# Reordering the start-up of a fused attention and gated-unit kernel: two load queues, evacuations between normalisations, casts behind masks

## The chip, the cores and the metric

One core of a Trainium2 chip runs the whole kernel. The metric is the time of one execution in microseconds (us), as the device reports it; a profiled execution gives the span, some 1.8 us shorter. The kernel before took 198.24 us (median of 3 runs, 197.85 to 199.29). Single runs of one kernel differ by about 1% here, and some fall in a slower state; ratios use fast runs alone.

## The reference, cut to what matters

```python
# q, k, v: (8 batches, 8 heads, 576, 64) float32
scores = scale * np.matmul(q, k.transpose(0, 1, 3, 2))
scores = np.where(pos[:, None] // 64 >= pos[None, :] // 64, scores, -1e9)   # block-causal
attn   = softmax(scores)                        # over the last axis
x      = (attn @ v), heads side by side         # (8, 576, 512)
gate   = sigmoid(causal convolution of x with 5 taps per channel)
out    = (gate * (x @ w_val)) @ w_out           # w_val, w_out: (512, 512)
```

## The kernel before

The program is software-pipelined by hand: nothing is reordered by a scheduler, each engine runs its instructions in the order in which the source emits them, and a tile layer adds the semaphores. A step `p` is one pair of heads (32 steps, 4 per batch). It computes the scores of pair `p`, the value products of pair `p - 1`, the transposes of pair `p + 1`, and from step 5 on parts of the gated unit of an earlier batch (convolution, `val`, and output tiles).

576 positions are 4 blocks of 128 and a *tail* of 64. The tails of all 8 heads of a batch are loaded together, cast to fp16 by GpSimd (`cast_tails`), transposed by TensorE (`trans_tails`) and evacuated by VectorE, once in 4 steps. The other pieces are the mask and the order of emission:

```python
def mask(p):                       # zeroes the forbidden corners of exp(scores)
    pt = pts[p % NPT]              # written by ScalarE's exponential (line 188)
    nc.gpsimd.memset(pt[64:128, ...], 0.0)
    nc.gpsimd.memset(pt[64:128, 0:2, 896:960], 0.0)

def casts(p):                      # all on GpSimd, ahead of mask(p)
    for i in (p + 1, p + 2):
        if i < NP and i not in qkT and i not in qk16 and (p >= 5 or i == p + 1):
            cast_qk(i)
    cast_v(p)
    if p % 4 == 0:
        cast_vtail(p // 4)
    if p == 3 or (p > 0 and p % 4 == 0 and p + 4 < NP):
        cast_tails((p + 4) // 4, nc.gpsimd)
    if p in (6, 7):
        cast_w_out(p - 6)

for p in range(NP):
    # ... (cv: a step with a convolution) ...
    loads(p)
    casts(p)
    s_tile(p, 0)                   # scores: matmuls, then one exponential each
    s_tile(p, 1)
    # ... p == 0 cut ...
    av(p - 1, ...)                 # value products and normalisation, both heads
    trans(p + 1, 2)                # 8 transposes (TensorE), evacuation (VectorE)
    # ... out(3) from step 11; permutations of w_out ...
    s_tile(p, 2)
    mask(p)
    # ... s_last, conv ...
    xtrans(p - 1, ...)
    # ... scale_w_val in steps 5 and 6, val twice ...
    if p == 3 or (p > 0 and p % 4 == 0 and p + 4 < NP):
        trans_tails((p + 4) // 4, 1)     # last thing of TensorE's step
```

The softmax here doesn't subtract the row's maximum and nothing guards it: scores larger than these inputs give would overflow.

## Time and profile before

| stretch | TensorE busy | step length | what it does |
|---|---|---|---|
| 0 to 8 us | partly, with fillers | | first loads, casts, transposes |
| 8 to 31 us, steps 0 to 4 | 8.1 of 10 us from 20 to 30 us | 3.7 to 4.3 us from step 1 | attention alone |
| 31 to 67 us, steps 5 to 11 | 8.4 to 9.2 of 10 us | 4.4 to 6.5 us | attention and gated unit, no output until step 11 |
| 67 to 166 us, steps 12 to 31 | all of it | 4.7 to 5.7 us | all stages |
| 166 to 197 us | nearly all of it | | remaining gates and outputs |

A step's length is taken here from the start of its first exponential on ScalarE to the start of the next step's, read off the timeline. From the page of the kernel before, the 40-slice rows (each digit is a busy share in tenths; PEclk is the granted TensorE clock) and the chain that ended last:

```profile
PE   2999878779899999999999999999999999999992
...
PEclk9999999999999999999999999999999999999998
DMA  5999999999899568876887687977775111124445
...
PE 80%; DVE 10%; POOL 3%; ACT 2%; DMA 2%; issue 1%; POOLq 0%; SPq 0%; DVEq 0%; ACTq 0%
```

TensorE is full from about a third of the way, and the chain is 80% TensorE. In the first third it is not, and DMA is at 9 tenths there.

### The profile page before, as it was taken

Reading aid. Unit: us, or ns where it says so; the run is one execution under the profiler, and the core shown is the slowest. Engines: PE = TensorE matmul, PEld = TensorE weight load, DVE = VectorE, ACT = ScalarE, POOL = GpSimd, SP = SyncE. Lnnn points to the kernel's source line nnn. Section 1 sums busy time; section 2 is a strip of 40 time slices with the busy share of each in tenths; the row PEclk is TensorE's granted clock in tenths of the full one; section 3 lists DMA queues with packets and bytes.
Section 4 is the critical chain, followed back from the end, with each engine's and each line's share of the span. In section 5 each row is a group of like instructions: output and inputs, shape, how many; then the busy total and the mean of one; then the engine's idle time right before and its main releaser. Section 6 shows DMA issues by size and latency. Waiting matters only on the chain.

```text
span 196.6 us, 8730 instructions
## 1 busy us (share of the span) xinstructions
PE 183.3 (93%) x3714; PEld 124.4 (63%) x3714; DVE 130.8 (67%) x286; ACT 138.6 (71%) x192; POOL 83.5 (42%) x168
## 2 busy tenths in 40 slices
PE   2999878779899999999999999999999999999992
PEld 1456656557577676667766677677767676755550
DVE  4346785897678686777686877768676868642451
ACT  4438778758699778877888878887988787635321
POOL 7363664596444554345434644464445422100000
PEclk9999999999999999999999999999999999999998
DMA  5999999999899568876887687977775111124445
GB/s 155 256 286 265 250 274 323 312 215 278 242 224 253 171 174 217 255 228 186 236 232 234 189 240 212 276 216 207 220 213 146 57 56 58 58 107 165 163 160 213
DMA packets 70337, 40.43 MB, mean 206 GB/s; under 512 B 48149, under 2 KB 64789, under 8 KB 70298
## 3 DMA queue, kind: packets, MB, share of 16 engines
q1 hardware_dynamic: 69872, 39.46, 73.8%
q8 instruction: 29, 0.48, 1.0%
q10 hardware_dynamic: 426, 0.40, 0.6%
q14 instruction: 10, 0.08, 0.2%
HBM read 30.42 MB, written 9.44 MB: 203 GB/s over the span
## 4 chain that ended last, share of the span: by engine, by line
PE 80%; DVE 10%; POOL 3%; ACT 2%; DMA 2%; issue 1%; POOLq 0%; SPq 0%; DVEq 0%; ACTq 0%
PE G L33 51%; PE S L33 18%; PE G L154 6%; PE G L244 5%; DVE qkT L165 3%; DVE x L235 3%; DMA vs<-in_v_dram 2%; POOL qk L129 1%; ACT pt L188 1%; PE G L141 1%; DVE w_val L379 1%; DVE rc L234 1%; DVE gv L282 1%; POOL v L134 1%; POOL pt L204 1%
## 5 line engine op out<-in xcount | busy, mean ns | idle before, releaser
L188 ACT ACTIVATE pt<-S 128x1024 f16<-128x1024 f32 x96 | 95.0, 1024 | 21.4 <-PE S L33 19.1
L204 POOL MEMSET pt<- 64x384 f16 x32 | 13.5, 423 | 74.0 <-ACT pt L188 73.9
L33 PE MATMUL G<-xt,w_val 128*128 128x288 f16 x256 | 37.9, 286 | 0.3 <-DVE qkT L165 0.2
L165 DVE COPY qkT<-G 128x1024 f16<-128x1024 f16 x31 | 37.7, 1215 | 0.2 <-PE G L154 0.2
L129 POOL CAST qk<-qks 128x1024 f16<-128x1024 f32 x31 | 32.9, 1061 | 10.9 <-DMA qks<-in_k_dram 7.7
L33 PEld LDWEIGHTS <-pt 128*128 128x128 f16 x960 | 31.2, 97 | 8.6 <-issue 4.0
L33 PE MATMUL G<-w_out,gv 128*128 128x512 f16 x144 | 36.5, 379 | 0.0
L33 PE MATMUL G<-v,pt 128*128 128x65 f16 x896 | 34.1, 194 | 1.7 <-DVE gv L282 1.3
L282 DVE SCALAR_TENSOR_TENSOR gv<-th,G 128x288 f16<-128x288 f32 x64 | 28.2, 453 | 10.7 <-PE G L33 9.0
L304 ACT COPY osb<-G 128x512 f32<-128x512 f32 x31 | 18.2, 586 | 23.8 <-PE G L33 22.0
L235 DVE TENSOR_TENSOR x<-G,rc 128x320 f16<-128x320 f32 x64 | 31.5, 492 | 2.2
L33 PEld LDWEIGHTS <-qkT 64*128 64x128 f16 x496 | 16.0, 94 | 22.9 <-issue 16.8
L33 PE MATMUL S<-qkT 64*128 64x512 f16 (+1 forms) x248 | 28.5, 301 | 2.1 <-DVE qkT L165 1.1
L33 PEld LDWEIGHTS <-w_val 128*128 128x128 f16 x256 | 24.2, 98 | 8.5 <-issue 0.9
L234 DVE RECIPROCAL rc<-G 128x5 f32<-128x5 f32 x64 | 12.2, 190 | 22.6 <-PE G L33 22.5
L246 DVE COPY xt<-G 128x576 f16<-128x576 f16 x32 | 14.6, 455 | 13.5 <-PE G L244 13.2
L154 PE MATMUL G<-ident,qk 128*128 128x128 f16 x256 | 20.1, 222 | 0.2 <-POOL qk L129 0.2
L134 POOL CAST v<-vs 128x512 f16<-128x512 f32 x32 | 19.9, 621 | 0.5 <-DMA vs<-in_v_dram 0.3
L33 PEld LDWEIGHTS <-gv 128*128 128x128 f16 x144 | 12.9, 98 | 9.9
L33 PE MATMUL G<-xt,DG 32*32 32x288 f16 x640 | 17.2, 288 | 0.0
L33 PE MATMUL S<-xt,DG 32*32 32x288 f16 x640 | 17.1, 287 | 0.0
L154 PEld LDWEIGHTS <-qk 128*128 128x128 f16 x256 | 15.4, 100 | 1.3 <-POOL qk L129 0.4
(58 smaller groups left out, 151.8 us busy)
## 6 DMA issues: line engine op xcount, KB each, us to landing
out_dram<-osb SPq DMA_DIRECT2D x35, 256.0 KB, 2.1
qks<-in_q_dram SPq DMA_DIRECT2D x32, 256.0 KB, 4.2
vs<-in_v_dram SPq DMA_DIRECT2D x64, 128.0 KB, 4.4
qks<-in_k_dram SPq DMA_DIRECT2D x31, 256.0 KB, 4.3
tlst<-in_q_dram SPq DMA_DIRECT2D x8, 128.0 KB, 4.8
tlst<-in_k_dram SPq DMA_DIRECT2D x8, 128.0 KB, 4.6
vtst<-in_v_dram SPq DMA_DIRECT2D x8, 128.0 KB, 4.8
w_st<-in_moe_w_val_dram SPq DMA_DIRECT2D x2, 512.0 KB, 6.3
```

The costliest lines, as they stand in the source:

```text
L33: nc.tensor.matmul(out=out, lhsT=lhsT, rhs=rhs, start=start, stop=stop, skip_group_check=True)
L129: nc.gpsimd.tensor_copy(out=o, in_=s)
L134: nc.gpsimd.tensor_copy(out=v16s[p % NV][0:128, 0:4, 0:2, 0:64], in_=s)
L154: nc.tensor.transpose(out=r[:, o:o + 128], in_=t[0:128, c, 2 * i:2 * i + 2, 0:64], identity=ident16[0:128, 0:128])
L165: nc.vector.tensor_copy(out=o[0:128].rearrange("p i (s n) -> p i s n", n=4), in_=src)
L188: nc.scalar.activation(out=pts[p % NPT][0:128, 0:2, 512 * t:512 * t + 512], in_=s[0:128, 0:2, 0:512], func=AF.Exp, bias=0.0, scale=0.125)
L204: nc.gpsimd.memset(pt[64:128, 0:2, 0:1536].rearrange("p h (t s) -> p h t s", t=3)[:, :, :, 0:64], 0.0)
L234: nc.vector.reciprocal(out=rc[0:128], in_=O[:, :, 64:65])
L235: nc.vector.tensor_tensor(out=x[0:128, 0:5, h, 0:64], in0=O[:, :, 0:64], in1=rc[0:128].to_broadcast([128, 5, 64]), op=ALU.mult)
L246: nc.vector.tensor_copy(out=xts[b % NX][0:128, g, 4:4 + SEQ], in_=r[:, 0:SEQ])
L282: nc.vector.scalar_tensor_tensor(out=gv[u][0:128, x, bi, hf, 0:288], in0=t[0:128, x, 0:288], scalar=1.0, in1=r[0:128, 0:288], op0=ALU.add, ...
L304: nc.scalar.copy(out=o[0:128], in_=r[0:128, 0:512])
```

## The change

Intent: begin earlier and keep VectorE and GpSimd from holding TensorE in the first third. The parts are: first loads on two queues and the first transposes in two PSUM banks; in steps 1 to 4 the evacuation of the transposes between the two normalisations; query/key casts only one tile ahead until step 9; tail and weight casts behind the mask; tail loads later; gate matmuls spread over the step, output tiles from step 12 instead of 11.

```diff
+    load_tails(0)                       # k half now on ScalarE's queue
+    nc.scalar.dma_start(out=conv_nat[0:5, 0:512], in_=moe_conv_w[:, :])
+    load_v1(0, nc.scalar)
     tiny = const([128, 1], fp32, "tiny")
... cut: casts of tile 0 both on VectorE, transposes of tile 0 in banks 2 and 0,
... av() split into av() and norm(), conv() with the score bank's tanh first
     def loads(p):
-        if b + 2 < B and m == 2:
+        if b + 2 < B and m == 3 and b > 0:
             load_tails(b + 2)
...
+    def tails(p):
+        if p in (3, 7):
+            return p // 3
+        return p // 4 + 1 if p > 4 and p % 4 == 0 and p + 4 < NP else None
+
     def casts(p):
...
-            if ... (p >= 5 or i == p + 1):
+            if ... (p >= 9 or i == p + 1):
...
-        if p == 3 or (p > 0 and p % 4 == 0 and p + 4 < NP):
-            cast_tails((p + 4) // 4, nc.gpsimd)
-        if p in (6, 7):
-            cast_w_out(p - 6)
+
+    def mask_and_tails(p):
+        mask(p)
+        if tails(p):
+            cast_tails(tails(p), nc.gpsimd)
+        if p in (7, 8):
+            cast_w_out(p - 7)
...
+    for p in range(LAG):                # steps 0 to 4
...
+        if p > 1:
+            xtrans(p - 2, 3)
+        av(p - 1, 0, 0)
+        norm(p - 1, 0, 0)
+        av(p - 1, 1, 1)
+        trans(p + 1, 2)
+        norm(p - 1, 1, 1)
+        s_tile(p, 2)
+        mask_and_tails(p)
...
+        if tails(p):
+            trans_tails(tails(p), 0)    # still at the end of the same step
... cut: steps 5 to 31 likewise; scale_w_val 0 to 3 all in step 6; fillers 26 -> 13
```

More of the change, by code (lines that the diff above doesn't have):

```diff
@@ L94, in load_tails @@
         for o, src in ((0, q), (64, k)):
-            nc.sync.dma_start(out=t[o:o + 64, 0:8, 0:64],
+            (nc.scalar if b == 0 and o else nc.sync).dma_start(
+                              out=t[o:o + 64, 0:8, 0:64],
                               in_=src[b, 0:8, 512:576, 0:64].rearrange("h s d -> s h d"))
@@ L100, in load_vtail, with load_v1 @@
                           in_=v[b, 0:8, 512:576, 0:64].rearrange("h s d -> s h d"))
-    def load_v1(p):
+    def load_v1(p, eng=None):
         b, g = divmod(p, 4)
@@ L105, in load_v1 @@
         for h in range(2):
-            nc.sync.dma_start(
+            (eng or nc.sync).dma_start(
                 out=t[0:128, 0:4, h, 0:64],
@@ L125, in cast_qk @@
         if first:
-            nc.scalar.copy(out=o[:, 0:2], in_=s[:, 0:2])
+            nc.vector.tensor_copy(out=o[:, 0:2], in_=s[:, 0:2])
             nc.vector.tensor_copy(out=o[:, 2:4], in_=s[:, 2:4])
@@ L148, in trans @@
     def trans(p, bank=None):
-        r = gbank(bank)[0:128].bitcast(fp16)
         t = qk16.pop(p)
+        banks = (2, 0) if p == 0 else (bank, bank)
+        rr = [GT[i][0:128].bitcast(fp16) for i in banks]
         for i in range(2):
@@ L153, in trans @@
                 o = 512 * i + 128 * c
-                nc.tensor.transpose(out=r[:, o:o + 128], in_=t[0:128, c, 2 * i:2 * i + 2, 0:64],
+                nc.tensor.transpose(out=rr[i][:, o:o + 128], in_=t[0:128, c, 2 * i:2 * i + 2, 0:64],
                                     identity=ident16[0:128, 0:128])
-        src = r.rearrange("p (i n s) -> p i s n", i=2, n=4)
+        src = [r.rearrange("p (i n s) -> p i s n", i=2, n=4) for r in rr]
         if p == 0:
             o = [const([128, 512], fp16, f"qk0_{i}")[0:128] for i in range(2)]
-            nc.scalar.copy(out=o[0].rearrange("p (s n) -> p s n", n=4), in_=src[:, 0])
-            nc.vector.tensor_copy(out=o[1].rearrange("p (s n) -> p s n", n=4), in_=src[:, 1])
+            nc.scalar.copy(out=o[0].rearrange("p (s n) -> p s n", n=4), in_=src[0][:, 0])
+            nc.vector.tensor_copy(out=o[1].rearrange("p (s n) -> p s n", n=4), in_=src[1][:, 1])
             qkT[p] = o
@@ L164, in trans @@
             qkT[p] = [o[0:128, i] for i in range(2)]
-            nc.vector.tensor_copy(out=o[0:128].rearrange("p i (s n) -> p i s n", n=4), in_=src)
+            nc.vector.tensor_copy(out=o[0:128].rearrange("p i (s n) -> p i s n", n=4), in_=src[0])
     def s_tile(p, t):
@@ L211, with av @@
     x16 = {}
-    def av(p, banks):
+    def av(p, h, bank):
         b, g = divmod(p, 4)
@@ L216, in av, with norm, avs @@
         vv = v16s[p % NV]
-        x = p2.tile([128, 5, 2, 64], fp16, tag="x16", name="x16")
-        x16[p] = x
-        for h in range(2):
-            r = gbank(banks[h])
-            for i in range(5):
-                for j in range(i + 1):
-                    if j == 4:
-                        o = 64 * (4 * h + g)
-                        l = pt4[b % 2][0:128].rearrange("p a s -> p (a s)")[:, o:o + 128]
-                        w = v16t[b % 2][0:128, 2 * g + h, 0:65]
-                    else:
-                        o = 1280 + 64 * j if i == 4 else off[j] + 128 * i
-                        l = pt[0:128, h, o:o + 128]
-                        w = vv[0:128, j, h, 0:65]
-                    mm(r[0:128, 65 * i:65 * i + 65], l, w, start=(j == 0), stop=(j == i))
-            O = r[0:128, 0:325].rearrange("p (i d) -> p i d", d=65)
-            rc = p2.tile([128, 5, 1], fp32, tag="rc", name="rc")
-            nc.vector.reciprocal(out=rc[0:128], in_=O[:, :, 64:65])
-            nc.vector.tensor_tensor(
-                out=x[0:128, 0:5, h, 0:64], in0=O[:, :, 0:64],
-                in1=rc[0:128].to_broadcast([128, 5, 64]), op=ALU.mult)
+        r = gbank(bank)
+        for i in range(5):
+            for j in range(i + 1):
+                if j == 4:
+                    o = 64 * (4 * h + g)
+                    l = pt4[b % 2][0:128].rearrange("p a s -> p (a s)")[:, o:o + 128]
+                    w = v16t[b % 2][0:128, 2 * g + h, 0:65]
+                else:
+                    o = 1280 + 64 * j if i == 4 else off[j] + 128 * i
+                    l = pt[0:128, h, o:o + 128]
+                    w = vv[0:128, j, h, 0:65]
+                mm(r[0:128, 65 * i:65 * i + 65], l, w, start=(j == 0), stop=(j == i))
+    def norm(p, h, bank):
+        if h == 0:
+            x16[p] = p3.tile([128, 5, 2, 64], fp16, tag="x16", name="x16")
+        O = GT[bank][0:128, 0:325].rearrange("p (i d) -> p i d", d=65)
+        rc = p2.tile([128, 5, 1], fp32, tag="rc", name="rc")
+        nc.vector.reciprocal(out=rc[0:128], in_=O[:, :, 64:65])
+        nc.vector.tensor_tensor(
+            out=x16[p][0:128, 0:5, h, 0:64], in0=O[:, :, 0:64],
+            in1=rc[0:128].to_broadcast([128, 5, 64]), op=ALU.mult)
+    def avs(p, banks):
+        for h in range(2):
+            av(p, h, banks[h])
+            norm(p, h, banks[h])
     def xtrans(p, bank=None):
@@ L249, with conv @@
     th = {}
-    def conv(n, banks=(None, None)):
+    def conv(n, banks=(None, None), score_first=False):
         b, hf = divmod(n, 2)
@@ L264, in conv @@
                        start=(kk == 0), stop=(kk == 4))
-        for row in (2, 3):
-            nc.scalar.activation(out=t[0:128, row, 0:288], in_=rr[row][:, 0:288],
-                                 func=AF.Tanh, bias=0.0, scale=0.5)
-        nc.scalar.activation(out=t[0:128, 0:2, 0:288], in_=s[0:128, 0:2, 0:288],
-                             func=AF.Tanh, bias=0.0, scale=0.5)
+        for part in ((0, 2, 3) if score_first else (2, 3, 0)):
+            if part == 0:
+                nc.scalar.activation(out=t[0:128, 0:2, 0:288], in_=s[0:128, 0:2, 0:288],
+                                     func=AF.Tanh, bias=0.0, scale=0.5)
+            else:
+                nc.scalar.activation(out=t[0:128, part, 0:288], in_=rr[part][:, 0:288],
+                                     func=AF.Tanh, bias=0.0, scale=0.5)
     def val(n, x, bank=None):
@@ L311 @@
     nc.scalar.activation(out=tiny[0:128], in_=tiny[0:128], func=AF.Exp, bias=0.0, scale=1.0)
-    nc.scalar.dma_start(out=conv_nat[0:5, 0:512], in_=moe_conv_w[:, :])
-    load_tails(0)
     make_identity(nc, ident)
+    wz = const([128, 512], fp16, "wz")
+    nc.vector.memset(wz[0:128], 0.0)
     nc.vector.tensor_copy(out=ident16[0:128], in_=ident[0:128])
@@ L321 @@
     load_qk1(1)
-    load_v1(0)
     load_vtail(0)
@@ L338, with warm @@
         nc.gpsimd.memset(xts[i][0:128, 0:4, 0:4], 0.0)
-    wz = const([128, 512], fp16, "wz")
-    nc.vector.memset(wz[0:128], 0.0)
-    wr = gbank(1)
-    def warm(n):
+    def warm(n, bank=1):
         for _ in range(n):
-            mm(wr[0:128, 0:512], wz[0:128, 0:128], wz[0:128])
+            mm(GT[bank][0:128, 0:512], wz[0:128, 0:128], wz[0:128])
     warm(4)
@@ L349 @@
     trans(0)
-    warm(3)
+    warm(2)
     cast_tails(0, nc.vector)
@@ L395, in loads @@
             load_v1(p + 3)
-        if p == 0:
-            load_tails(1)
+        if p in (0, 4):
+            load_tails(1 + p // 4)
         if b + 1 < B and m == 1:
@@ L403, in loads @@
             load_w_out(p - 3)
+    def tails(p):
+        if p in (3, 7):
+            return p // 3
+        return p // 4 + 1 if p > 4 and p % 4 == 0 and p + 4 < NP else None
     def casts(p):
         for i in (p + 1, p + 2):
-            if i < NP and i not in qkT and i not in qk16 and (p >= 5 or i == p + 1):
+            if i < NP and i not in qkT and i not in qk16 and (p >= 9 or i == p + 1):
                 cast_qk(i)
@@ L428 @@
     LAG = 5
-    for p in range(NP):
-        gs = p - LAG
-        cv = gs >= 0 and gs % 2 == 0
+    for p in range(LAG):
         loads(p)
@@ L437 @@
         if p == 0:
-            warm(3)
+            warm(2)
             trans_tails(0, 0)
-        else:
-            av(p - 1, (0, 1) if cv or gs < 0 else (1, 0))
-        if 0 < p < NP - 1:
+            s_tile(0, 2)
+            mask(0)
+            trans(1, 2)
+            warm(2)
+            s_last(0)
+            warm(1, 3)
+            conv_weights()
+            continue
+        if p > 1:
[3 more added lines that the diff above has]
+        av(p - 1, 1, 1)
@@ new lines @@
+        trans(p + 1, 2)
+        norm(p - 1, 1, 1)
+        s_tile(p, 2)
+        mask_and_tails(p)
+        if p == 1:
+            warm(2, 3)
+        if tails(p):
+            trans_tails(tails(p), 0)
+        if p == 4:
+            s_last(1)
+    for p in range(LAG, NP):
+        gs = p - LAG
+        cv = gs % 2 == 0
+        early = p < 12
+        h = gs - 1
+        loads(p)
+        casts(p)
+        if p == 6:
+            scale_w_val(0)
+            scale_w_val(1)
+        s_tile(p, 0)
+        s_tile(p, 1)
+        if p == LAG:
+            xtrans(p - 2, 3)
+        avs(p - 1, (0, 1) if cv else (1, 0))
+        if p < NP - 1:
@@ L443 @@
             trans(p + 1, 2)
-        if p in (8, 9, 10):
-            permute_w_out({8: 0, 9: 2, 10: 3}[p], 3)
-        if p > 10:
+        if not early:
             out(3)
-        if p == 0:
-            warm(3)
+        elif gs > 0:
+            val(h // 2, 2 * (h % 2), 3)
         s_tile(p, 2)
-        mask(p)
-        if p % 4 == 2 and p > 2 and p + 2 < NP:
+        mask_and_tails(p)
+        if p == 8 or (p % 4 == 2 and p > 6 and p + 2 < NP):
             s_last((p + 2) // 4)
-        if p == 0:
-            warm(2)
-            conv_weights()
-            warm(3)
-            trans(1, 2)
-            s_last(0)
-            warm(5)
@@ L461 @@
-        if cv:
-            conv(gs // 2, (0, 1))
-        if p > 0:
-            xtrans(p - 1, 2 if cv else 3 if gs < 0 else 0)
-        if p == 1:
-            warm(3)
-        if p in (5, 6):
-            scale_w_val(2 * p - 10)
-            scale_w_val(2 * p - 9)
+        if cv:
+            conv(gs // 2, (0, 1), early)
+        xtrans(p - 1, 2 if cv else 0)
         if gs > 0:
-            h = gs - 1
-            val(h // 2, 2 * (h % 2), 3)
-            val(h // 2, 2 * (h % 2) + 1, 0 if cv else 2)
+            if not early:
+                val(h // 2, 2 * (h % 2), 3)
+            val(h // 2, 2 * (h % 2) + 1, 3 if early and cv else 1 if early else 0 if cv else 2)
@@ L474 @@
             if h % 2 == 1:
                 complete(h // 2)
-        if p == 8:
-            permute_w_out(1, 1)
-        if p == 3 or (p > 0 and p % 4 == 0 and p + 4 < NP):
-            trans_tails((p + 4) // 4, 1)
-        if p == 4:
-            s_last(1)
-    av(NP - 1, (1, 0))
+        if p == 6:
+            scale_w_val(2)
+            scale_w_val(3)
+        if 9 <= p <= 11:
+            permute_w_out({9: 0, 10: 1, 11: 3}[p], 2)
+        if p == 10:
+            permute_w_out(2, 3)
+        if tails(p):
+            trans_tails(tails(p), 2 if cv else 3 if early else 1)
@@ L485 @@
+    avs(NP - 1, (1, 0))
     ring[0] = 2
```

## The prediction

> **What bounds the kernel now.** Three stretches. (1) From about 67 us to 193 us TensorE is the limit: the slices of the page show it 99% busy, and the chain of waits is 80% PE. The change does not touch the work there. (2) From 7.6 to 67 us it is not: the windows show PE 8.1 to 9.2 us busy in each 10 us, and "busy" includes 26 filler matmuls. Steps 1 to 4 take 3.75 us each: the timeline shows a ring of key/query evacuation (1.21 us, VectorE), score matmuls (0.6), first value product (0.65), two normalisations (1.36), evacuation again. Steps 5 to 8 take 5.1 to 5.9 us for 3.8 to 4.7 us of TensorE work. (3) Under it lies DMA: its share is 0.96 to 1.21 of 16 engines in every 10 us window from 10 to 60 us; GpSimd waited 2.4 and 2.1 us for query/key loads at 33.6 and 38.3 us, and its late mask then held up the value products (0.6 and 1.6 us).
>
> **What the change does, costed.**
> - Start: query cast to VectorE; two PSUM banks let ScalarE and VectorE evacuate at once (before: 6.27 and then 6.88 us). About 0.6 us. The second queue brings no bandwidth (Trainium skill, "DMA: Bandwidth & Descriptors", Issuing engines are not separate DMA queues: all run on the same 16 DMA engines and interleave; here the share is already full from 2.3 us).
> - Step 0: the second transposes no longer wait behind the convolution weights and 8 fillers. Second step's scores at about 11.7 us, not 14.3.
> - Steps 1 to 4: the evacuation comes between the normalisations, so one of them (0.68 us) hides behind the next scores. About 3.2 us a step, near ScalarE's 3 x 1.02 us. Step 5 would start near 25 us, not 29.5.
> - Steps 5 to 11: one query/key cast ahead instead of two, casts behind masks, gates split, tanh of the score bank first: removes the GpSimd waits. The four weight scalings (0.9 us each, VectorE) now all lie in step 6. One output tile (0.86 us) moves from step 11 to the tail: no gain.
>
> **How much lands.** VectorE and ScalarE savings run into DMA. Its order is the same but for the tail loads, which move later; the same bytes must come. From the landings of before (query/key tiles 6, 7, 8 at 29.5, 33.5, 38.2 us) less one tail load of 1.2 us, steps 6, 7, 8 cannot start before about 31, 35 and 40 us (before: 34.3, 39.9, 46.3). The fourth batch's tails now come after tile 10 and must be cast and transposed at the end of step 8: landing about 46.5 us, so step 9 starts about 47.7 us (52.1 before). Steps 9 to 11 take about as long as before (15 us less the output tile, plus a permutation or two). So step 12 starts about 62.5 instead of 67.2 us; less the 0.86 us of the moved output tile, 3.8 us are gained.
>
> **Prediction: 194.4 us**, range 191.5 to 196.8; faster by over 2% 0.47, within 2% 0.50, slower 0.03.
>
> **What would show it.** Scores of step 1 at 11 to 12.5 us; steps 2 to 4 of 3.1 to 3.4 us; the evacuation between two reciprocals on VectorE; GpSimd's longest DMA waits moved to tail casts (46 us) or query/key casts of steps 5 to 7; DMA share over 0.95 until 47 us; an unchanged 10.4 us per two steps after 70 us; a tail longer by about 0.9 us.
>
> **What would make it wrong.** If DMA moves the early bytes faster, step 9 starts near 45 us and the time is 191 to 192. If VectorE's 7.5 us of work in step 6 or a cold TensorE (half the fillers) stalls steps, it is 196 or more.

## More of the kernel before

GpSimd in step 12 of the kernel before, from the timeline (start in us, length in us, engine, line, operation, tiles, and in brackets idle time before it and its releaser):

```profile
68.89 0.62 POOL L115 CAST tl<-tlst 128x512 f16<-128x512 f32 x1
71.80 0.41 POOL L204 MEMSET pt<- 64x384 f16 x1 [2.28 <-ACT pt L188]
72.15 0.20 POOL L206 MEMSET pt<- 64x128 f16 x1
```

The tail cast (line 115) is done at 69.5 us. Then GpSimd waits for ScalarE's last exponential of the step and clears the mask until 72.35 us. TensorE at the end of that step, same view:

```profile
70.80 1.14 PE L33 MATMUL G<-xt,w_val 128*128 128x288 f16 x8
71.78 0.39 PE L141 MATMUL G<-ident,tl 128*128 128x128 f16 x4
72.10 0.61 PE L33 MATMUL S<-qkT 64*128 64x512 f16 x6
```

The tail transposes (line 141) follow the gate matmuls without a gap, and the next scores follow them. Over the whole run, TensorE's waits for the tails' cast (view of the tail tile, TensorE's two lines of it; us in total, times) were:

```profile
  PEld L141: 0.6, 1
  PE G L141: 0.4, 1
```

Finally, the ring of step 2 in the kernel before, from the timeline:

```profile
18.21 0.20 POOL L206 MEMSET pt<- 64x128 f16 x1
...
18.47 1.04 POOL L129 CAST qk<-qks 128x1024 f16<-128x1024 f32 x1
...
19.57 0.62 PE L154 MATMUL G<-ident,qk 128*128 128x128 f16 x8
...
20.47 1.21 DVE L165 COPY qkT<-G 128x1024 f16<-128x1024 f16 x1
```

The mask ends at 18.41, the query/key cast follows, TensorE's transposes start 0.06 us after the cast's end, and the evacuation 0.28 us after they end (the second normalisation stood before it).

## The result, and the profile after

The changed kernel took **205.69 us** (median of 4 runs, 205.11 to 206.41), against 198.76 us for the kernel before in the same comparison: ratio 1.0355, 95% interval 1.0295 to 1.0415. It is slower, and the prediction was wrong in its direction and outside its range. (A ratio is the mean time of one kernel's fast runs over the mean of the other's fast runs of the same rounds, so it is not quite the ratio of the medians quoted.)

The page after, the same rows:

```profile
PE   4897598899699979997999979997999999999992
...
PEclk9999969999999999999999999999999999999999
DMA  5999999997999476596766987597378111124455
...
PE 75%; DMA 6%; ACT 6%; POOL 4%; DVE 3%; issue 2%; SPq 2%; ACTq 0%; POOLq 0%; DVEq 0%
```

TensorE is no longer full in the last two thirds: a 7 recurs every four or five slices (a batch of four steps lasts four), and the granted clock falls to 6 tenths in the sixth slice. The lengths of the steps that differ (us, first exponential to first exponential):

| step | before | after | difference |
|---|---|---|---|
| 0 (with its start) | 14.69 | 13.30 | -1.39 |
| 1 | 3.74 | 3.39 | -0.35 |
| 2 | 3.81 | 3.92 | +0.11 |
| 3 | 3.74 | 5.72 | +1.98 |
| 4 | 4.25 | 5.32 | +1.07 |
| 5 to 11 together | 37.44 | 37.51 | +0.07 |
| 12 | 4.91 | 6.12 | +1.21 |
| 16 | 4.91 | 6.34 | +1.43 |
| 20 | 4.91 | 6.23 | +1.32 |
| 24 | 4.91 | 6.23 | +1.32 |
| from step 31's first exponential to the end | 30.71 | 31.55 | +0.84 |

All other steps from 13 on agree within 0.02 us. The sum is 7.61 us, which is the difference of the profiled spans (204.2 - 196.6 = 7.6). Every steady step that lost has a tail cast in it, so the answer is in the lines that were shown above. GpSimd in step 12 after:

```profile
73.17 0.41 POOL L206 MEMSET pt<- 64x384 f16 x1 [3.37 <-ACT pt L190]
73.52 0.20 POOL L208 MEMSET pt<- 64x128 f16 x1
73.79 0.61 POOL L116 CAST tl<-tlst 128x512 f16<-128x512 f32 x1
```

The cast of the tails (line 116) now stands behind the mask, so it starts at 73.79 us instead of 68.89. And TensorE:

```profile
72.17 1.14 PE L33 MATMUL G<-xt,w_val 128*128 128x288 f16 x8
74.46 0.40 PE L142 MATMUL G<-ident,tl 128*128 128x128 f16 x4 [1.14 <-POOL tl L116]
74.79 0.61 PE L33 MATMUL S<-qkT 64*128 64x512 f16 x6
```

TensorE had reached the tail transposes by 73.3 us and stood still for 1.14 us, although the next step's scores only needed an evacuation that VectorE had finished at 72.31:

```profile
71.10 1.21 DVE L167 COPY qkT<-G 128x1024 f16<-128x1024 f16 x1
```

The waits over the whole run, view of the tail tile:

```profile
  PEld L142: 10.9, 7
...
  PE G L142: 8.9, 7
```

From one wait of 0.4 us, TensorE's own waits for this cast went to 8.9 us in 7 places (10.9 us counted at its weight loads, whose waits overlap these). The Trainium skill, "TensorE: Matmul & The Clock Gate", Step-by-step: what each phase is for, says that only weight loads are pulled ahead and matmuls stay in program order. This trace agrees as to the matmuls: the six score matmuls that were ready did not pass the four transposes that were not.

### The profile page after: what moved, and what is told of

It is laid out like the page before. It is cut to its first block, busy times and chain, and to the rows that moved or that the text cites. A ratio compares the mean times of both kernels' runs of the same rounds, so it can differ in the third digit from the quotient of the medians.

```text
span 204.2 us, 8697 instructions
## 1 busy us (share of the span) xinstructions
PE 183.6 (90%) x3701; PEld 124.5 (61%) x3701; DVE 132.3 (65%) x287; ACT 137.7 (67%) x191; POOL 83.1 (41%) x168
## 4 chain that ended last, share of the span: by engine, by line
PE 75%; DMA 6%; ACT 6%; POOL 4%; DVE 3%; issue 2%; SPq 2%; ACTq 0%; POOLq 0%; DVEq 0%
PE G L33 45%; PE S L33 17%; PE G L156 7%; PE G L252 5%; DMA qks<-in_k_dram 5%; ACT pt L190 4%; POOL tl L116 2%; DMA vs<-in_v_dram 2%; SPq L86 1%; PE G L142 1%; DVE qkT L167 1%; ACT osb L314 1%; POOL pt L208 1%; ACT L324 1%; SPq L107 1%
## 5 line engine op out<-in xcount | busy, mean ns | idle before, releaser
L33 PE MATMUL G<-xt,w_val 128*128 128x288 f16 x256 | 38.5, 286 | 0.0
L33 PEld LDWEIGHTS <-pt 128*128 128x128 f16 x960 | 32.2, 99 | 7.0 <-issue 4.9
L33 PE MATMUL G<-v,pt 128*128 128x65 f16 x896 | 34.8, 195 | 1.0 <-issue 0.6
L130 POOL CAST qk<-qks 128x1024 f16<-128x1024 f32 x31 | 32.3, 1045 | 5.0 <-DMA qks<-in_k_dram 3.6
L156 PE MATMUL G<-ident,qk 128*128 128x128 f16 x256 | 20.6, 225 | 2.1 <-DVE qk L127 1.8
L135 POOL CAST v<-vs 128x512 f16<-128x512 f32 x32 | 20.9, 654 | 0.9 <-DMA vs<-in_v_dram 0.8
```

What stands on the lines that cost most here:

```text
L33: nc.tensor.matmul(out=out, lhsT=lhsT, rhs=rhs, start=start, stop=stop, skip_group_check=True)
L130: nc.gpsimd.tensor_copy(out=o, in_=s)
L135: nc.gpsimd.tensor_copy(out=v16s[p % NV][0:128, 0:4, 0:2, 0:64], in_=s)
L156: nc.tensor.transpose(out=rr[i][:, o:o + 128], in_=t[0:128, c, 2 * i:2 * i + 2, 0:64], identity=ident16[0:128, 0:128])
```

## The experiments

Twelve kernels ran, all correct against the reference. "Clear of noise" below means that the 95% interval of the ratio excludes 1. Two theories were set against each other first: M, that the cast behind the mask makes TensorE wait in order, and D, that the moved tail loads land too late.

### a_tails_first: that part undone

```diff
 def casts(p):
+    if tails(p):
+        cast_tails(tails(p), nc.gpsimd)
 def mask_and_tails(p):
     mask(p)
-    if tails(p):
-        cast_tails(tails(p), nc.gpsimd)
```

> The changed kernel with one part undone: GpSimd casts the tails ahead of the step's mask again; their load stays late. Theory M (the cast waits behind a mask that waits for ScalarE, and TensorE waits in order for the cast): steps 12, 16, 20, 24 fall from 6.1-6.3 back to 4.9 us, TensorE's waits for the tail cast from 10.9 to under 1.5 us, step 3 loses its 1.9 us excess, and the time falls by 7 to 9 us, to 197-199. Rival D (the tails land too late because their load was moved): nothing changes, GpSimd shows DMA waits at the tail cast, time stays near 205.

Measured: 199.88 us (4 runs, 197.93 to 200.58), ratio to before 1.0051 (0.9987 to 1.0115). Step 12 is 4.81 us and steps 16, 20 and 24 are 4.91 or 4.92 us again, step 3 is 3.85 and step 4 is 4.10. The span of its profiled run (its fastest) is 196.1 us, 8.1 us under the changed kernel's. GpSimd in its step 12:

```profile
66.95 0.62 POOL L116 CAST tl<-tlst 128x512 f16<-128x512 f32 x1
70.41 0.41 POOL L206 MEMSET pt<- 64x384 f16 x1 [2.83 <-ACT pt L190]
```

The cast is back in the time in which GpSimd waits for the exponential anyway. The load stayed late and 5.4 us of steady loss still went, so D is out as the main cause. TensorE's waits for the cast fell from 8.9 to 1.8 us (2.2 us at its weight loads, more than the 1.5 expected); 1.63 us of that lie in step 8, where the cast did wait for its late load (tf_load3 below). The slowdown is undone, but with it gone the other parts of the change are not clear of noise.

### b_tails_behind: that part alone, in the kernel before

```diff
 casts(p):
-    if p == 3 or (p > 0 and p % 4 == 0 and p + 4 < NP):
-        cast_tails((p + 4) // 4, nc.gpsimd)
 loop:
     mask(p)
+    if p == 3 or (p > 0 and p % 4 == 0 and p + 4 < NP):
+        cast_tails((p + 4) // 4, nc.gpsimd)
```

> The kernel before with that one part done alone: the tails are cast behind the mask. Theory M: steps 4, 8, 12, 16, 20, 24 and 3 lengthen, the four steady ones by 1.2 to 1.4 us each; time up by 5 to 9 us, to 203-207. If the slowdown came from the other parts of the change, the time stays within 1 us of 198.5.

Measured: 208.45 us (207.80 to 208.75), ratio 1.0494 (1.0458 to 1.0530). Steps 12, 16, 20 and 24 are 6.23, 6.28, 6.23 and 6.72 us. Who waited for the tails:

```profile
  PEld L141: 11.3, 7
...
  PE G L141: 9.3, 7
```

So this one move is enough for the whole slowdown and more; the loss is even above the range given (203 to 207), because steps 3, 4 and 5 lost 1.7, 2.3 and 1.2 us and the clock fell to between 0.66 and 0.84 in the windows from 25 to 40 us. Undoing it and doing it alone agree, and the cause is shown.

### a_trans_next_step: the late cast kept, the transposes moved

```diff
-        if tails(p):
-            trans_tails(tails(p), ...)             # end of step p
+        if tails(p - 1):
+            trans_tails(tails(p - 1), ...)         # step p, behind s_tile(p, 1)
```

> The changed kernel, tails still cast behind the mask, but TensorE transposes them one step later, behind the next step's first score matmuls. Theory M (it is TensorE's in-order wait that costs, not the place of the cast on GpSimd): steady steps back to 4.9 us, time 197-199.5, as a_tails_first. If the late cast itself delays GpSimd's later casts and masks (rival G), steps 13, 17, 21, 25 get longer and the time stays above 201.

Measured: 202.22 us (201.10 to 204.45), ratio 1.0145 (1.0096 to 1.0193): of the changed kernel's excess over a_tails_first (1.0355 - 1.0051) about two thirds came back. The time and the longer step 13 (6.44 us, 5.55 in a_tails_first) are what rival G expected, not M; but the wait behind them is M's. TensorE in step 13:

```profile
72.63 0.61 PE L33 MATMUL S<-qkT 64*128 64x512 f16 x6
73.84 0.40 PE L142 MATMUL G<-ident,tl 128*128 128x128 f16 x4 [0.61 <-POOL tl L116]
```

The six score matmuls in between last 0.6 us, and the cast ends 1.2 us after they begin, so TensorE still waited 0.61 us. Steps 12 and 13 together took 11.02 us here, 10.36 in a_tails_first and 11.67 in the changed kernel: of the 0.66 us that are left, 0.61 are this wait, so G is not needed for the steady steps. Step 4 took 6.43 us, against 4.10 in a_tails_first, with a wait of 0.94 us for the cast and then half clock from 25.48 to 28.89 us (the next experiment is about that). This form is part of a cure: the move has to be longer than the wait. Whether a still later place would cure all of it was not run.

### a_fill: was the slow step 4 a second wait or the clock?

```diff
         if tails(p):
+            warm(9, 0)                  # 9 matmuls on zeros, about 2 us
             trans_tails(tails(p), 0)    # first loop: step 3 alone
```

> The changed kernel with 9 filler matmuls (about 2 us) in TensorE's 2.5 us wait for the tail cast at the end of step 3. If the wait also let the granted clock fall (0.83 between 20 and 30 us; 65-column matmuls nearly twice as slow in step 4), step 4 falls from 5.32 to about 4.1 us while step 3 stays at 5.7, and the time falls by about 1.2 us. If the slow step 4 comes from the waits themselves and not from the clock, step 4 stays at 5.3.

Measured: step 3 stays at 5.73 us and step 4 falls from 5.32 to 3.86 us; the time is 204.23 us, ratio 1.0280 (1.0244 to 1.0317) against 1.0355 for the changed kernel (the two intervals overlap a little, so it is the steps of the profile that carry the argument). The windows, one us each (the columns are: window, its length, busy time and count of PE, PEld, DVE, ACT and POOL, then the granted clock, DMA share and GB/s), of the changed kernel:

```profile
23.00:24.00 1.00, 0.00 (x0) 0.00 (x0) 1.00 (x2) 0.92 (x1) 0.00 (x0) 1.00 1.04 285
...
27.00:28.00 1.00, 1.00 (x22) 1.00 (x20) 0.63 (x2) 1.00 (x2) 0.56 (x2) 0.50 1.08 319
```

and of a_fill:

```profile
23.00:24.00 1.00, 1.00 (x7) 0.47 (x5) 0.96 (x3) 0.81 (x1) 0.07 (x1) 1.00 0.92 303
...
27.00:28.00 1.00, 1.00 (x29) 0.89 (x27) 0.78 (x4) 0.98 (x2) 0.27 (x1) 1.00 1.05 375
```

In the changed kernel TensorE stood still for 2.53 us from 22.99, and from about 26.6 to 30 us the clock was 0.50: fourteen 65-column matmuls took 0.96 to 0.98 us, against 0.59 in a_fill. With fillers in the same wait the clock stayed at 1.00. So step 3 paid for the wait, and step 4 paid again for its echo. The Trainium skill, "TensorE: Matmul & The Clock Gate", What's actually happening, has these two states, half clock after idleness and full clock after a busy window; the trace agrees as to the states (0.50 and 1.00), but not as to the length of idleness, of which more at the end.

### tf_casts2, tf_order, best1_order: the ring of steps 1 to 4

The prediction gave 3.2 us for these steps, and 3.4 to 3.9 us were measured where no tail cast interfered. The changed kernel's step 2, timeline:

```profile
19.17 1.02 ACT L190 ACTIVATE pt<-S 128x1024 f16<-128x1024 f32 x1 [0.54 <-PE S L33]
...
20.67 0.20 POOL L208 MEMSET pt<- 64x128 f16 x1
...
20.93 1.04 POOL L130 CAST qk<-qks 128x1024 f16<-128x1024 f32 x1
...
22.03 0.62 PE L156 MATMUL G<-ident,qk 128*128 128x128 f16 x8
...
22.69 1.23 DVE L167 COPY qkT<-G 128x1024 f16<-128x1024 f16 x1 [0.28 <-PE G L156]
```

The evacuation does stand between the normalisations now. But it starts right when the transposes end, the transposes start 0.06 us after the query/key cast ends, that cast follows the mask, and the mask follows the exponential. This is the same ring as in the kernel before. Another path of the same length goes over TensorE's order: scores, x transposes, both value products, and only then the transposes (the last value product starts at 21.91 us, 0.12 us before them). Three kernels, all on top of a_tails_first, cut one, both, or the other:

```diff
 # tf_casts2 (GpSimd's part): two tiles ahead, so ahead of the mask
-            ... (p >= 9 or i == p + 1):
+            ... (p >= 9 or p < 4 or i == p + 1):
 # tf_order (both): the same for 0 < p < 4, and TensorE's order
-        if p > 1:
-            xtrans(p - 2, 3)
         av(p - 1, 0, 0)
         norm(p - 1, 0, 0)
-        av(p - 1, 1, 1)
         trans(p + 1, 2)
+        av(p - 1, 1, 1)
         norm(p - 1, 1, 1)
+        if p > 1:
+            xtrans(p - 2, 3)
 # best1_order (TensorE's part): the order alone, on top of best1 below
```

> a_tails_first, and in steps 0 to 3 the query/key cast runs two tiles ahead, so it stands before the mask on GpSimd. Theory P (the ring that sets steps 1 to 4 goes exponential, mask, cast, transposes, evacuation, scores; so moving normalisations on VectorE gained nothing): steps 2 to 4 fall from 3.9 to 3.2-3.5 us, and 1 to 2 us are kept at step 5. Rival V (the ring goes over value products and TensorE's order: scores, x transposes, value products, transposes, evacuation = 3.86 us): steps 2 to 4 stay at 3.8-3.9 us.

> a_tails_first with both rings of steps 1 to 4 shortened: transposes between the two value products and x transposes last on TensorE, and query/key casts two tiles ahead in steps 1 to 3, so before the mask. My reckoning: steps 2 to 4 of 3.1 to 3.4 us instead of 3.9, so step 5 begins 1 to 1.8 us earlier. If DMA (query/key landings) bounds these steps, they stay at 3.8 or more on average and GpSimd shows waits for query/key loads of more than 3 us beyond the first.

> best1 with TensorE's order changed in steps 1 to 4 (transposes between the value products, x transposes last), casts not moved. If the ring over TensorE's order alone sets these steps, steps 2 to 4 fall from 3.9 to 3.1-3.4 us. If the ring over mask and query/key cast on GpSimd is as long (the trace has the transposes 0.06 us after the cast), steps 2 to 4 stay at 3.7-3.9 us.

| steps | after | a_tails_first | tf_casts2 | tf_order | best1_order |
|---|---|---|---|---|---|
| 1 | 3.39 | 3.40 | 3.60 | 3.11 | 3.12 |
| 2 | 3.92 | 3.92 | 3.83 | 3.63 | 4.41 |
| 3 | 5.72 | 3.85 | 4.32 | 5.85 | 5.89 |
| 4 | 5.32 | 4.10 | 3.86 | 4.99 | 5.30 |
| time, us | 205.69 | 199.88 | 198.20 | 199.31 | 199.40 |
| ratio | 1.0355 | 1.0051 | 0.9977 | 1.0021 | 1.0017 |

The expectations for tf_casts2 came out as the rival's: cutting GpSimd's part alone does next to nothing (0.09 us in step 2; its step 3 has a tail wait of 1.22 us). Cutting TensorE's part alone (best1_order) is enough in step 1, but makes step 2 worse, because TensorE now meets the transposes before the cast is done (it waited 0.62 us) with the second value product behind them. Its step 3 has the same wait, but most of its excess is the clock, which was 0.50 from 21.92 to 25.33 us. Cutting both (tf_order) gave 3.11 and 3.63 us in steps 1 and 2, so in step 2 each path alone holds the step. Then step 3 gave all of it back. GpSimd in tf_order:

```profile
22.76 1.04 POOL L130 CAST qk<-qks 128x1024 f16<-128x1024 f32 x1 [2.04 <-DMA qks<-in_k_dram]
...
24.30 0.62 POOL L116 CAST tl<-tlst 128x512 f16<-128x512 f32 x1
```

The cast two tiles ahead waited 2.04 us for its load (tile 5 had not landed before 22.7 us), and the tail cast stood behind it, so TensorE waited 2.2 us for the tails again, and the clock fell to 0.66 between 25 and 30 us. Here it is the late load, in the place where the order exposes TensorE to it, that sets the limit. None of the three is clear of the kernel before.

### tf_scalepool: VectorE's load in step 6

```diff
-        nc.vector.tensor_scalar(out=w_val_sb...)      # all four in step 6
+        nc.gpsimd.tensor_scalar(out=w_val_sb...)      # two in step 5, two in 6, ahead of the mask
```

> a_tails_first with the four weight scalings on GpSimd in steps 5 and 6, before the mask, instead of VectorE in step 6 (3.4 us of its time there). If VectorE's load in step 6 holds the value products, steps 5 to 7 together fall from 15.73 to 14.2-15.2 us. If not, they stay within 0.3 us or grow because the mask comes later.

Measured: steps 5 to 7 took 15.82 us against 15.72 in a_tails_first, 198.08 us in all, ratio 0.9965 (0.9924 to 1.0006). A miss, and not a clean test: on GpSimd the scalings put the mask off, and TensorE waited 0.43 and 0.80 us for the mask in these steps, where a_tails_first has no such wait. So the scalings on VectorE are not shown to hold these steps, nor ruled out. What bounds step 7 (5.8 to 6.6 us in all versions) was not settled.

### tf_load3 and best1: does the tails' load matter at all?

Rival D was out as the main cause, but in a_tails_first one tail cast did wait for its load:

```profile
48.48 0.61 POOL L116 CAST tl<-tlst 128x512 f16<-128x512 f32 x1 [2.37 <-DMA tlst<-in_k_dram]
```

```diff
 # tf_load3, on top of a_tails_first: the fourth batch's tails loaded in step 6 again
-        if b + 2 < B and m == 3 and b > 0:
+        if b + 2 < B and m == (2 if b == 1 else 3) and b > 0:
 # best1, on top of tf_load3: the output-weight casts ahead of the mask as well
```

> a_tails_first with the fourth batch's tails loaded in step 6, as in the kernel before. In a_tails_first GpSimd waited 2.4 us for them at 48.5 us and TensorE 1.6-1.9 us for the cast. If the late load is the cause, step 8 falls from 5.86 to 4.2-4.8 us and step 9 from 6.24 to about 5.4 (the weight and query/key casts come earlier), and the time falls by 1.5 to 2.5 us, to 196.5-198. If DMA is simply full there, another load is late by as much, and the start of step 10 moves by less than 0.7 us.

> tf_load3 with the two output-weight casts also moved ahead of the mask on GpSimd (in tf_load3 the second one, behind the mask at 48.6 us, pushed the query/key cast and TensorE waited 0.73 us for it). If casts behind masks are the common cause, step 9 falls from 6.15 to 5.0-5.5 us and the time to 195.3-196.3. If not, step 9 stays over 6 us.

tf_load3: 196.62 us (196.09 to 197.00), ratio 0.9902 (0.9870 to 0.9934), faster than the kernel before and clear of noise, though by less than 2%. Step 8 fell from 5.86 to 4.49 us as expected; step 9 went only from 6.24 to 6.15. GpSimd there:

```profile
45.69 0.62 POOL L116 CAST tl<-tlst 128x512 f16<-128x512 f32 x1
...
48.63 1.04 POOL L394 CAST w<-w_st 128x1024 f16<-128x1024 f32 x1
```

The tails are now cast without a wait at 45.69, and the weight cast is the one behind the mask. best1 moved that too: 196.10 us (195.15 to 200.06, the last a slow run), ratio 0.9870 (0.9834 to 0.9907). Step 9 became 5.90, not the 5.0 to 5.5 expected. TensorE is busy for 5.42 us of it, and its waits over 0.1 us sum to 0.41. In its profiled run GpSimd waited for loads instead:

```profile
47.14 0.61 POOL L116 CAST tl<-tlst 128x512 f16<-128x512 f32 x1 [1.61 <-DMA tlst<-in_k_dram]
...
50.94 1.04 POOL L130 CAST qk<-qks 128x1024 f16<-128x1024 f32 x1 [0.49 <-DMA qks<-in_k_dram]
```

The first of these put off the mask and the query/key cast that TensorE waited for, so DMA stands behind the little wait that is left; for most of step 9 TensorE has work. The intervals of tf_load3 and best1 overlap; best1's further gain is not shown.

### best2 and best3: the start again

```diff
 # best2 = best1_order, casts two tiles ahead in steps 1 and 2 only
 # best3 = best2, and:
-    load_v1(0, nc.scalar)            # ahead of the first activation
     nc.scalar.activation(out=tiny..., func=AF.Exp)
+    load_v1(0, nc.scalar)
... conv_weights() moved from step 0 to step 1
```

> best1_order with query/key casts two tiles ahead in steps 1 and 2 only (in tf_order the one of step 3 waited 2 us for its load and held the tail cast behind it). Both rings are cut: steps 2 and 3 of 3.1 and 3.6 us as in tf_order, step 4 of 3.7-4.1 instead of 5.85; step 5 begins 0.8 to 1.5 us before best1's; the time 0.5 to 1.5 us under best1's. If DMA takes it back (tile 6 lands at about 28 us whatever the order), step 7 begins within 0.4 us of best1's.

> best2 with the first exponential's table load ahead of ScalarE's load of v, and the convolution weights made at the end of step 1 instead of step 0. ScalarE was held to 5.2 us by five DMA issues and then loaded the table for 1.3 us, so step 0's first exponential should start 0.4 to 0.7 us earlier and step 1 0.5 to 1 us earlier. If DMA bounds steps 5 to 8 the gain is gone by step 7; else the time is 0.3 to 1 us under best2's.

best2: 196.77 us (ratio 0.9907, 0.9871 to 0.9943); its profiled run fell in the slow state (its 512-column fillers still took 0.61 to 0.63 us at 19.8 us, against 0.38 from 10.8 us on in the changed kernel), so its steps are not read. best3: 196.93 us (ratio 0.9909, 0.9868 to 0.9950). In best3 step 1 began at 12.46 us, against 13.04 in best1, and step 4 at 23.15 against 24.20; but step 4 took 5.29 us, against 4.10, and step 5 began at 28.44 against 28.30. TensorE waited 0.60 us in step 4 for the query/key cast, which is one tile ahead again there. So 1 us was given back within one step. The earlier start is not shown to come from the edit either: with the start unchanged, step 1 began between 12.61 and 13.56 us in the fast profiled runs. Neither version beats best1.

The best versions, 0.9 to 1.3% faster than the kernel before, are thus tf_load3, best1, best2 and best3, whose intervals overlap. The simplest is tf_load3: the changed kernel with its tail casts ahead of the mask again and one load put back.

## Why the prediction was wrong, point by point

- **"From about 67 us to 193 us TensorE is the limit ... The change does not touch the work there."** This step failed. The work is the same, but the order is not: one line in the casts applies to every batch, and it cost 1.2 to 1.4 us in steps 12, 16, 20 and 24 each, 5.3 of the 7.6 us. (Another 3.05 us went in steps 3 and 4, and the earlier start gave 1.39 us back.)
- **"casts behind masks ... removes the GpSimd waits."** This is the term that had the wrong sign. Moving a cast behind the mask frees the mask, but hangs the cast on the step's last exponential; its consumer on TensorE had stayed at the end of the same step. Waits for this cast went from 0.4 to 8.9 us. The diff alone could tell it: GpSimd's mask waits for ScalarE in the profile before (73.9 us in total), and `trans_tails` was still in the same step.
- **Steps 1 to 4 of "about 3.2 us".** Wrong: 3.4 and 3.9 us in steps 1 and 2, 3.85 in step 3 without the tail wait. The ring was read as VectorE's, with 0.68 us to save; but the normalisations held the evacuation for only 0.28 us in the step shown above, a path over mask and query/key cast was as long, and TensorE's order made another. tf_order shows that in step 2 both must be cut.
- **The start: "About 0.6 us", scores of step 1 "at about 11.7 us".** The direction was right, the sizes were not. The first exponential came 0.23 us earlier, not 0.6 (0.2 to 0.5 us earlier in the other fast profiled runs with this start), and step 1's scores at 12.87 us. The two banks did their part, but ScalarE issued five loads first, as its lines after show:

```profile
3.04 2.10 ACTq L107 DMA_DIRECT2D vs<-in_v_dram  x2
5.17 1.28 ACT L324 ACT_TABLE_LOAD   x1 [5.17 <-DMA qks<-in_k_dram]
...
6.57 0.57 ACT L161 COPY qk<-G 128x512 f16<-128x512 f16 x1
```

  The table load began at 5.17 us (1.28 in the kernel before), so ScalarE's evacuation could not start before 6.57, though VectorE had started its own at 6.00. Step 1's scores then waited for the convolution weights' matmuls, which TensorE did from 11.89 to 12.94 us.
- **"The second queue brings no bandwidth."** Right: 213 GB/s in the first 10 us after, 208 before, at a share of 0.88 in both. That is what the page of the skill that the prediction names says.
- **DMA as the limit of steps 6 to 8.** Wrong in the changed kernel: after the first wait of 3.6 us GpSimd waited for no query/key load, nor in a_tails_first, where steps 6 to 8 still began at 33.2, 37.9 and 44.1 us and not at 31, 35 and 40; what held them there was not settled. The tail load of the fourth batch "landing about 46.5 us" holding step 9 was the right mechanism in a_tails_first (the cast began at 48.48 us after a 2.37 us wait) and tf_load3 confirms it; in the changed kernel itself the mask came later than the load (52.07 us) and hid it.
- **"a tail longer by about 0.9 us".** Right: 0.84 us, the output tile that moved from step 11 to the end.
- **"a cold TensorE (half the fillers) stalls steps".** Half right: the clock did fall in step 4, but after the 2.5 us wait in step 3, and fillers put into that wait kept the clock at 1.00. The start was colder too: 512-column fillers still took 0.63 us at 8.56 us, where the kernel before took 0.38 (the PEclk rows do not show this, because the traces hold no clock record before 9.5 and 7.5 us). What that cost was not separated.

The gain that was expected, where the cast is put right, mostly did not appear either: a_tails_first is level with the kernel before. Its first 13 steps gain 1.4 us in the profiled run, and 0.9 us of this goes to the tail.

## What to carry to other kernels

When an instruction moves down one engine's queue, look up what it now waits behind, and then where its consumer stands in the queue of the engine that is the limit: if the consumer did not move as far, the limit engine pays the difference at every repetition. Search the whole run for the repetitions of an edit that is meant for the start. A ring that several engines close at nearly the same length is not shortened by cutting it on one of them, and a wait of TensorE should be costed with the slow clock that can follow it.

## What the Trainium skill lacked or had wrong

- "TensorE: Matmul & The Clock Gate" (What's actually happening, and the table under Why this matters for your kernels) gives about 3.4 us of idleness, or gaps over about 3 us, for a return to half clock. Here one gap of 2.53 us was enough in the changed kernel, and two, of 0.99 and 0.94 us, in a_trans_next_step. In five kernels the clock fell in mid-run, six times in all, and each time for 3.41 us; the 3.41 us before were not idle: TensorE was busy for 1.08 us of them in the changed kernel, 1.48 in a_trans_next_step and 2.09 in best1_order. (The page's section A second HAM failure mode: psum-queue depth-cycling does know such falls after short idle times between groups of matmuls, but gives no busy share for them.) Which share is enough is not shown: after 1.66 us (best3, 33.84 to 37.25 us) no fall followed. Windows of best1_order, columns as above, with no wait of a matmul over 0.62 us between 17 and 22 us:

```profile
20.00:21.00 1.00, 0.57 (x10) 0.29 (x10) 0.35 (x1) 1.00 (x2) 0.58 (x3) 1.00 1.27 263
21.00:22.00 1.00, 0.46 (x15) 0.33 (x12) 0.47 (x2) 1.00 (x2) 1.00 (x2) 0.96 1.36 219
22.00:23.00 1.00, 0.93 (x10) 0.93 (x11) 0.22 (x1) 0.07 (x1) 1.00 (x3) 0.50 1.01 212
```

- "DMA: Bandwidth & Descriptors" (Issuing engines are not separate DMA queues) calls the time that it takes to issue a DMA usually small beside the DMA, and gives no figure there for what it costs the engine that issues. Here each of five loads took 0.38 to 0.98 us to issue on ScalarE's queue, and together they held its first table load until 5.17 us, against 1.28 us in the kernel before.
- No page that was read puts a number on one engine's in-order wait for a late producer: 7 tail casts cost the changed kernel 8.9 us of TensorE, of which 1.14 us in step 12.
